# Interleaved channels and a plain load of x in a convolution and gated feed-forward kernel on Trainium2

## The chip, the cores and the metric

The kernel runs on one core of one Trainium2 chip. The metric is the time of one execution on the device in microseconds (us), the median of several runs. The profile belongs to one further execution; its span runs from the first to the last instruction.

## The reference

The input x has 8 sequences of 4096 tokens with 192 channels. Eight heads of 24 channels each have seven taps, made positive and normalised by a softmax. Each channel is convolved along the tokens, causally, with its head's taps. The result goes through two matrix products with an activation between them, 192 to 2048 to 192:

```python
w = weight - np.max(weight, axis=-1, keepdims=True)
w = np.exp(w)
w = w / (np.sum(w, axis=-1, keepdims=True) + 1e-09)
x_pad = np.concatenate([np.zeros((B, K - 1, D)), x], axis=1)
x_unf = x_pad[:, idx, :].reshape(B, S, K, H, group)     # idx[s, k] = s + k
x = np.einsum('hk,bskhg->bshg', w, x_unf).reshape(B * S, D)
h = x @ w_in
g = h * (1.0 / (1.0 + np.exp(-beta * h)))
out = g @ w_out
```

All inputs and the output are float32; 32768 tokens in all.

## The kernel before

The tokens are cut into two streams of 16384 (NS = 2). Stream 0 lies on partitions 0 to 63, stream 1 on 64 to 127, so that a 64-row matmul of one stream runs beside one of the other. The 192 channels are three groups (NK = 3) of 64: group `kk` holds channels 64 kk to 64 kk + 63.

The work goes in steps over the tokens of both streams: 128, 128, 256, and then 31 steps of 512. A tile `j` is 512 tokens; the first three steps share tile 0. Step `i` runs 16 units (NF = 16 blocks of 128 hidden channels). In each unit `mm1` makes one block of h for step i (six matmuls, L257) and ScalarE's Silu writes it to `g` (L259), while `mm2` adds a share of the output of step i - 1 (L293), in an order laid out by `mm2_plan`. When a pair of 128-token blocks is complete, `store` copies it from PSUM on VectorE (L301, `o_sb`, four buffers) and SP stores it (L307). A step of 512 has four such pairs, complete near 6/16, 8/16, 14/16 and 16/16 of the following step. `last` does the second product of the last step alone (L316).

VectorE makes the convolution of step i + 1 during step i, two operations per unit from a list (`conv_ops`): a copy of the six last tokens of the tile before (`halo`, L220), then for each tap k and group kk one operation over n tokens, a multiply for k = 0 (L229) and a multiply-add for the others (L231); the last writes `xc` in bfloat16. The multiplier is a column of `taps3`, for which the head masks and sums the normalised taps of all heads.

x comes by `load_x`: eight DMAs per tile on POOL's queue, which cast to bfloat16 and put groups and streams in order (`x_bf`, three buffers). `transpose_x` issues four DMA transposes per tile on SP's queue (L104) into `xt`, three buffers, channels on partitions. Both are called at the start of a step: the transposes of tile j + 2, then the load of tile j + 3. Every DMA queue and every engine keeps the order of the program.

The head loads the first 128 tokens in float32 (`x0`), multiplies them with the taps on VectorE (L168) and sums seven shifted diagonal matmuls (L185) on TensorE for the `xc` of step 0. `w_in` is loaded with a cast by POOL's queue: columns 0 to 511 for both halves of the partitions, of the rest one half each, which SP's queue then copies to the other half (`copy_w_in`, L84). `w_out` is loaded in four parts and scaled by 1/beta on POOL (L207).

Of the kernel before, what the change touches and what calls it, by code (L numbers as in the profile page):

```python
# [10 lines left out]
FP32 = mybir.dt.float32  # L11
BF16 = mybir.dt.bfloat16
# [6 lines left out]
def kernel(  # L19
# [14 lines left out]
    group = D // H  # L34
# [3 lines left out]
    NK = D // 64  # L38
    NS = 2
    TS = B * S // NS  # L40
    TILE = 512

# [8 lines left out]
    xbf_pool = ctx.enter_context(tc.tile_pool(name="xbf", bufs=3))  # L51
# [13 lines left out]

    x0 = consts.tile([128, NS, D], FP32, name="x0")
    pin(nc.sync.dma_start(out=x0, in_=xs[:, 0:128, :].rearrange("s p d -> p s d")))
    wbc = consts.tile([128, H, K], FP32, name="wbc")
    pin(nc.sync.dma_start(out=wbc, in_=weight.rearrange("h k -> (h k)").partition_broadcast(128)))
    beta16 = consts.tile([NF, 128], FP32, name="beta16")  # L70
    pin(nc.sync.dma_start(out=beta16, in_=moe_beta.rearrange("(c p) -> c p", p=128)))

    w_in_s = consts.tile([128, NK, F], BF16, name="w_in_s")
    w_in_v = moe_w_in.rearrange("(k c) f -> c k f", c=64)
# [4 lines left out]
    def load_w_in(half, f0, f1):  # L79
        pin(nc.gpsimd.dma_start(out=w_in_s[64 * half:64 * half + 64, :, f0:f1], in_=w_in_v[:, :, f0:f1]))  # L80

    def copy_w_in(half, f0, f1):
        o = 1 - half
        pin(nc.sync.dma_start(out=w_in_s[64 * o:64 * o + 64, :, f0:f1],  # L84
                              in_=w_in_s[64 * half:64 * half + 64, :, f0:f1]))

    xbf_of, xt_of = {}, {}

    def load_x(j, b0=0, b1=4):
        if j not in xbf_of:  # L90
            xbf_of[j] = xbf_pool.tile([128, 4, NK, NS, 64], BF16, name="x_bf")
        t = xbf_of[j]
        for b in range(b0, b1):
            for s in range(NS):
                src = xs[s, TILE * j + 128 * b:TILE * j + 128 * (b + 1), :]
                pin(nc.gpsimd.dma_start(out=t[:, b, :, s, :],  # L96
                                        in_=src.rearrange("p (k c) -> p k c", c=64)))

    def transpose_x(j, b0=0, b1=4):
        if j not in xt_of:  # L100
            xt_of[j] = xt_pool.tile([128, NK, LEAD + TILE], BF16, name="xt")
        for b in range(b0, b1):
            c = LEAD + 128 * b
            pin(nc.sync.dma_start_transpose(  # L104
                out=xt_of[j][:, :, c:c + 128],
                in_=xbf_of[j][:, b, :, :, :].rearrange("p k s c -> p (k s c)")))

# [7 lines left out]


    load_w_in(0, 0, 512)
    load_w_in(1, 0, 512)
    shift = consts.tile([128, 128 + PAD], BF16, name="shift")
    pin(nc.gpsimd.memset(shift, 0.0))  # L120
    pin(nc.gpsimd.affine_select(out=shift, in_=shift, compare_op=ALU.not_equal, fill=1.0,
                                base=PAD, pattern=[[-1, 128 + PAD]], channel_multiplier=1))
# [4 lines left out]
    load_x(0, 0, 4)  # L127
    mask = consts.tile([128, NK, H], FP32, name="mask")
    pin(nc.gpsimd.memset(mask, 1.0))
    for s in range(NS):  # L130
        m = mask[64 * s:64 * s + 64, :, :]
        pin(nc.gpsimd.affine_select(out=m, in_=m, compare_op=ALU.is_ge, fill=0.0, base=0,  # L132
                                    pattern=[[64, NK], [-group, H]], channel_multiplier=1))
        pin(nc.gpsimd.affine_select(out=m, in_=m, compare_op=ALU.is_ge, fill=0.0, base=group - 1,  # L134
                                    pattern=[[-64, NK], [group, H]], channel_multiplier=-1))
    load_w_in(0, 512, 1024)
    load_w_in(1, 1024, 1536)
    load_w_in(0, 1536, 2048)
    load_x(1)

    for c in range(0, NF, 4):
        pin(nc.sync.dma_start(out=w_out_f[:, c:c + 4, :], in_=w_out_v[:, c:c + 4, :]))  # L142
        if c == 0:
            transpose_x(0, 0, 2)
            copy_w_in(0, 512, 1024)
        if c == 4:
            copy_w_in(1, 1024, 1536)
            transpose_x(0, 2, 4)
        if c == 8:
            copy_w_in(0, 1536, 2048)  # L150


    mx = consts.tile([128, H], FP32, name="mx")
    pin(nc.vector.tensor_reduce(out=mx, in_=wbc, axis=AX.X, op=ALU.max))
    pin(nc.vector.tensor_tensor(wbc, wbc, mx[:, :, None].to_broadcast([128, H, K]), ALU.subtract))
    pin(nc.scalar.activation(wbc, wbc, AF.Exp))
    pin(nc.scalar.activation(scrap, one, AF.Silu))
    sm = consts.tile([128, H], FP32, name="sm")
    pin(nc.vector.tensor_reduce(out=sm, in_=wbc, axis=AX.X, op=ALU.add))
    rs = consts.tile([128, H], FP32, name="rs")  # L160
    pin(nc.vector.reciprocal(rs, sm))
    taps = consts.tile([128, H, K], FP32, name="taps")
    pin(nc.vector.tensor_tensor(taps, wbc, rs[:, :, None].to_broadcast([128, H, K]), ALU.mult))


    xw = consts.tile([128, K, NS, D], BF16, name="xw")
    for k in range(K):
        pin(nc.vector.tensor_tensor(  # L168
            xw[:, k, :, :].rearrange("p s (h c) -> p s h c", c=group),
            x0.rearrange("p s (h c) -> p s h c", c=group),  # L170
            taps[:, None, :, k:k + 1].to_broadcast([128, NS, H, group]),
            ALU.mult))

    warm = psum_h.tile([128, 2, TILE], FP32, name="ph")
    for i in range(8):
        pin(nc.tensor.matmul(warm[:, i % 2, :], zeros[:, 0:128], zeros, start=True, stop=True))  # L176
    bps = psum_h.tile([128, 2, TILE], FP32, name="ph")
    pin(nc.tensor.transpose(bps[:, 0, 0:NF], beta16, id16))
    cva = psum_o.tile([128, 2, TILE], FP32, name="po")
    cvb = psum_o.tile([128, 2, TILE], FP32, name="po")  # L180
    cv = [cva[:, 0, 0:128], cva[:, 1, 0:128], cvb[:, 0, 0:128]]
    for k in range(K):
        for kk in range(NK):
            for s in range(NS):
                pin(nc.tensor.matmul(cv[kk][64 * s:64 * s + 64, :], xw[:, k, s, 64 * kk:64 * kk + 64],  # L185
                                     shift[:, k:k + 128], start=(k == 0), stop=(k == K - 1)))
    xc_of = {}
    xc_of[0] = xc_pool.tile([128, NK, TILE], BF16, name="xc")
    for kk in range(NK):
        pin(nc.scalar.activation(xc_of[0][:, kk, 0:128], cv[kk], AF.Copy))  # L190
# [6 lines left out]
    tmp3 = consts.tile([128, NK, K, H], FP32, name="tmp3")  # L197
    for kk in range(NK):
        pin(nc.vector.tensor_tensor(tmp3[:, kk, :, :],
                                    mask[:, kk:kk + 1, :].to_broadcast([128, K, H]),  # L200
                                    taps.rearrange("p h k -> p k h"), ALU.mult))
    taps3 = consts.tile([128, NK, K], FP32, name="taps3")
    pin(nc.vector.tensor_reduce(out=taps3, in_=tmp3, axis=AX.X, op=ALU.add))


    for c in range(NF):
        pin(nc.gpsimd.tensor_scalar_mul(w_out_s[:, c, :], w_out_f[:, c, :], rbeta[:, c:c + 1]))  # L207


    def conv_ops(i):  # L210
        t0, n = steps[i]
        j, c0 = t0 // TILE, t0 % TILE
        ops = []

        def halo():
            xt = xt_of[j]
            if t0 % S == 0 or t0 == 128:
                pin(nc.vector.memset(xt[:, :, LEAD - PAD:LEAD], 0.0))
            elif c0 == 0:
                pin(nc.vector.tensor_copy(xt[:, :, LEAD - PAD:LEAD], xt_of[j - 1][:, :, TILE + LEAD - PAD:]))  # L220

        def tap(kk, k):
            xt, xc = xt_of[j], xc_of[i]
            acc = accs[i]
            src = xt[:, kk, LEAD - PAD + c0 + k:LEAD - PAD + c0 + k + n]
            w = taps3[:, kk, k:k + 1]
            a = acc[:, kk, 0:n]
            if k == 0:
                pin(nc.vector.tensor_scalar_mul(a, src, w))  # L229
            else:  # L230
                pin(nc.vector.scalar_tensor_tensor(  # L231
                    out=xc[:, kk, 0:n] if k == K - 1 else a, in0=src, scalar=w, in1=a,
                    op0=ALU.mult, op1=ALU.add))

        def begin():
            xc_of[i] = xc_pool.tile([128, NK, TILE], BF16, name="xc")
            accs[i] = acc_pool.tile([128, NK, TILE], FP32, name="acc")
            if c0 == 0 or t0 == 128:
                halo()

        ops.append(begin)
        for k in range(K):
            for kk in range(NK):
                ops.append(lambda kk=kk, k=k: tap(kk, k))
        return ops

    accs, g_of, po_of = {}, {}, {}

    def mm1(i, fc):
        n = steps[i][1]
        ph = psum_h.tile([128, NS, TILE], FP32, name="ph")
# [69 lines left out]
    for i in range(n_steps):  # L323
# [3 lines left out]
        j = steps[i][0] // TILE  # L327
        if i == 1:
            transpose_x(1)
            load_x(2)  # L330
        elif i == 2:
            transpose_x(2)
            load_x(3)
# [44 lines left out]
```

## Time and profile before

| | |
|---|---|
| median of 3 runs | 715.21 us (714.91 to 715.98) |
| profiled execution | 712.91 us |
| its span | 711.2 us |
| granted TensorE clock | 0.999 |
| PE / ACT / DVE / POOL busy | 687.7 / 578.8 / 502.2 / 218.2 us |
| share of the 16 DMA engines, first four slices and after | 0.9 or more, then about 0.5 |

PE is TensorE, PEld its weight load, DVE VectorE, ACT ScalarE, POOL GpSimd, SP SyncE. A small q marks the engine's sequencer, which issues DMAs. In a group of instructions the columns are line, engine, operation, output <- inputs, shapes, count, then busy time and mean duration in ns, then idle time just before them and what ended it. In the list of waits they are the total, the number and the longest.

### The profile page before, as it was taken

The page shows a single profiled execution, that of the slowest core. Times are in us where ns is not written, and L with a number is a line of the kernel's source. Part 1 is how long each engine was busy: PE and PEld are TensorE (multiplying, and loading weights), DVE is VectorE, ACT ScalarE, POOL GpSimd, SP SyncE. Part 2 cuts the span into 40 slices and gives each one's busy share as a digit, 9 for nine tenths or more (in the row PEclk, how much of TensorE's full clock was granted, in tenths as well). Part 3 has the DMA queues.
Part 4 walks back from the last instruction along what each step waited for, and adds up shares of the span by engine and source line. Part 5 has one row for each costly group of instructions (what it writes and reads, how often), then busy time and mean ns, then how long its engine had stood idle before and what let it go on. Part 6 is the DMA issues. An engine that isn't in the chain of part 4 may idle for free.

```text
span 711.2 us, 25346 instructions
## 1 busy us (share of the span) xinstructions
PE 687.7 (97%) x11379; PEld 524.5 (74%) x11379; DVE 502.2 (71%) x877; ACT 578.8 (81%) x552; POOL 218.2 (31%) x290
## 2 busy tenths in 40 slices
PE   5589999999999999999999999999999999999998
PEld 2466777777777777777777777777777777777777
DVE  4779776677687667678667768766776876676702
ACT  3489888888888888888888888888888888888882
POOL 9997332223333113333212333321233330000000
PEclk9999999999999999999999999999999999999999
DMA  9999554455555445555445555544555553221012
GB/s 132 149 95 96 81 88 69 72 84 79 75 80 87 69 73 85 75 72 87 79 71 78 74 74 81 88 71 71 83 80 74 80 85 64 58 62 52 28 44 68
DMA packets 194861, 55.38 MB, mean 78 GB/s; under 512 B 158128, under 2 KB 194752, under 8 KB 194752
## 3 DMA queue, kind: packets, MB, share of 16 engines
q0 software_dynamic: 103440, 13.58, 30.6%
q1 hardware_dynamic: 91312, 40.17, 22.3%
q8 instruction: 89, 1.46, 0.9%
q14 instruction: 20, 0.16, 0.1%
HBM read 28.94 MB, written 25.17 MB: 76 GB/s over the span
## 4 chain that ended last, share of the span: by engine, by line
PE 93%; POOL 2%; DMA 2%; DVE 2%; issue 0%; ACT 0%; SPq 0%; DVEq 0%; POOLq 0%
PE ph L257 46%; PE po L293 46%; PE po L316 2%; DVE acc L231 1%; POOL x_bf L96 1%; DMA w_in_s<-w_in_s 1%; DMA x_bf<-in_x_dram 1%; POOL w_in_s L80 0%; ACT g L259 0%; DVE xc L231 0%; DVE acc L229 0%; SPq L142 0%; POOL mask L132 0%; POOL mask L134 0%; DVE o_sb L320 0%
## 5 line engine op out<-in xcount | busy, mean ns | idle before, releaser
L259 ACT ACTIVATE g<-ph,beta 128x1024 bf16<-128x1024 f32 (+2 forms) x544 | 574.9, 1064 | 111.8 <-PE ph L257 107.4
L257 PE MATMUL ph<-xc,w_in_s 64*128 64x512 bf16 (+2 forms) x3264 | 432.7, 367 | 17.0 <-DMA w_in_s<-w_in_s 9.4
L293 PEld LDWEIGHTS <-g 64*128 64x128 bf16 x7936 | 359.6, 94 | 101.5
L293 PE MATMUL po<-w_out_s,g 64*128 64x192 bf16 x7936 | 422.4, 243 | 0.0
L231 DVE SCALAR_TENSOR_TENSOR acc<-xt,taps,acc 128x512 f32<-128x512 bf16 (+2 forms) x495 | 326.7, 727 | 0.0
L96 POOL DMA_DIRECT2D x_bf<-in_x_dram x256 | 197.5, 774 | 366.7 <-DMA xt<-x_bf 349.4
L257 PEld LDWEIGHTS <-w_in_s 64*128 64x128 bf16 x3264 | 168.2, 96 | 74.6 <-DMA w_in_s<-w_in_s 10.5
L301 DVE COPY o_sb<-po 128x384 f32<-128x384 f32 x124 | 68.9, 556 | 183.5 <-PE po L293 183.5
L231 DVE SCALAR_TENSOR_TENSOR xc<-xt,taps,acc 128x512 bf16<-128x512 bf16 (+2 forms) x99 | 66.5, 727 | 0.0
L229 DVE TENSOR_SCALAR acc<-xt,taps 128x512 f32<-128x512 bf16 (+2 forms) x99 | 41.8, 481 | 9.2 <-DMA xt<-x_bf 8.1
L207 POOL TENSOR_SCALAR w_out_s<-w_out_f,rbeta 128x192 bf16<-128x192 f32 x16 | 15.6, 992 | 0.1
L316 PE MATMUL po<-w_out_s,g 128*128 128x192 bf16 x128 | 10.7, 246 | 0.0
L316 PEld LDWEIGHTS <-g 128*128 128x128 bf16 x128 | 10.5, 98 | 0.2 <-issue 0.2
L320 DVE COPY o_sb<-po 128x192 f32<-128x192 f32 x8 | 2.9, 358 | 7.6 <-PE po L316 7.6
L176 PE MATMUL ph<-zeros 128*128 128x512 bf16 x8 | 3.6, 631 | 1.2 <-DVE one L112 1.2
L220 DVE COPY xt<-xt 128x18 bf16<-128x18 bf16 x28 | 4.6, 166 | 0.0
L185 PE MATMUL po<-shift,xw 128*64 128x128 bf16 x42 | 3.3, 314 | 1.2 <-DVE xw L168 1.2
L185 PEld LDWEIGHTS <-xw 128*64 128x64 bf16 x42 | 2.0, 152 | 2.4 <-DVE xw L168 2.4
L80 POOL DMA_DIRECT2D w_in_s<-in_moe_w_in_dram x5 | 3.3, 665 | 0.8 <-POOLq L362 0.8
L168 DVE TENSOR_TENSOR xw<-x,taps 128x384 bf16<-128x384 f32 x7 | 3.4, 553 | 0.0
L176 PEld LDWEIGHTS <-zeros 128*128 128x128 bf16 x8 | 1.0, 140 | 2.9 <-issue 1.7
L190 ACT ACTIVATE xc<-po 128x128 bf16<-128x128 f32 x3 | 0.6, 278 | 3.1 <-PE po L185 3.1
(30 smaller groups left out, 8.8 us busy)
## 6 DMA issues: line engine op xcount, KB each, us to landing
out_dram<-o_sb SPq DMA_DIRECT2D x124, 192.0 KB, 2.3
x_bf<-in_x_dram POOLq DMA_DIRECT2D x256, 48.0 KB, 3.1
xt<-x_bf SPq DMA_TRANSPOSE x128, 2.3
w_out_f<-in_moe_w_out_dram SPq DMA_DIRECT2D x4, 384.0 KB, 6.7
w_in_s<-in_moe_w_in_dram POOLq DMA_DIRECT2D x5, 192.0 KB, 5.5
out_dram<-o_sb SPq DMA_DIRECT2D x8, 96.0 KB, 1.6
w_in_s<-w_in_s SPq DMA_DIRECT2D x3, 192.0 KB, 6.8
x<-in_x_dram SPq DMA_DIRECT2D x1, 192.0 KB, 2.6
```

The costliest lines, as they stand in the source:

```text
L96: pin(nc.gpsimd.dma_start(out=t[:, b, :, s, :], in_=src.rearrange("p (k c) -> p k c", c=64)))
L176: pin(nc.tensor.matmul(warm[:, i % 2, :], zeros[:, 0:128], zeros, start=True, stop=True))
L185: pin(nc.tensor.matmul(cv[kk][64 * s:64 * s + 64, :], xw[:, k, s, 64 * kk:64 * kk + 64], shift[:, k:k + 128], start=(k == 0), stop=(k == K ...
L207: pin(nc.gpsimd.tensor_scalar_mul(w_out_s[:, c, :], w_out_f[:, c, :], rbeta[:, c:c + 1]))
L220: pin(nc.vector.tensor_copy(xt[:, :, LEAD - PAD:LEAD], xt_of[j - 1][:, :, TILE + LEAD - PAD:]))
L229: pin(nc.vector.tensor_scalar_mul(a, src, w))
L231: pin(nc.vector.scalar_tensor_tensor(out=xc[:, kk, 0:n] if k == K - 1 else a, in0=src, scalar=w, in1=a, op0=ALU.mult, op1=ALU.add))
L257: pin(nc.tensor.matmul(ph[:, s, 0:n], w_in_s[r, kk, ts(fc, 128)], xc_of[i][r, kk, 0:n], start=(kk == 0), stop=(kk == NK - 1)))
L259: pin(nc.scalar.activation(g_of[i][:, fc, :, 0:n], ph[:, :, 0:n], AF.Silu, scale=beta[:, fc:fc + 1]))
L293: pin(nc.tensor.matmul(po[:, q, 0:D], g_of[i][r, fc, s, ts(b, 128)], w_out_s[r, fc, :], start=(phase == 0 and fc == 0), stop=(phase == 1 a ...
L301: pin(nc.vector.tensor_copy(o_sb, po[:, :, 0:D]))
L316: pin(nc.tensor.matmul(po[:, 0, 0:D], g_of[i][:, fc, s, ts(b, 128)], w_out_s[:, fc, :], start=(fc == 0), stop=(fc == NF - 1)))
```

## The change

Group `kk` now holds channels kk, kk + 3, kk + 6 and so on, so that partition q of a stream holds channels 3q, 3q + 1, 3q + 2, which belong to one head. One column of taps per partition then serves all three groups, and a tap becomes one VectorE operation over [128, 3, n]. The rows of `w_in` are read in the same interleaved order. The taps are loaded with one row per partition, exponentiated with a running sum, and normalised as `tapn`; the masks go.

x is loaded as float32, two DMAs per tile on SP's queue (for the first 256 tokens on ACT's queue), and cast and reordered on VectorE (`cast_x`, two operations per tile). Transposes stay on SP's queue; they are issued after the casts, at the end of VectorE's list of the step, and the load of the next tile comes behind them. The list of a step is spread over 14 units. In a steady step VectorE's order is: halo, two taps, first output copy, two taps, second output copy, three taps, two casts, third and fourth output copy. SP's is: three stores, four transposes, two loads, the fourth store.

The first 256 tokens are transposed on TensorE. The first 128 are convolved there: seven diagonal matrices of unnormalised taps in the 4-byte type fp32r, 21 matmuls, and ScalarE scales by the reciprocal of the sum as it copies. `w_in` columns 512 to 1023 are loaded for both halves, so two copies are left, and half of `w_out` is scaled on VectorE. The order of the loads in the head changes with it.

```diff
-    NK = D // 64
+    NK = 3
+    Q = D // NK
...
-    xbf_pool = ctx.enter_context(tc.tile_pool(name="xbf", bufs=3))
+    xf_pool = ctx.enter_context(tc.tile_pool(name="xf", bufs=2))
+    xbf_pool = ctx.enter_context(tc.tile_pool(name="xbf", bufs=2))
...
-    def load_x(j, b0=0, b1=4):
-        for b in range(b0, b1):
-            for s in range(NS):
-                src = xs[s, TILE * j + 128 * b:TILE * j + 128 * (b + 1), :]
-                pin(nc.gpsimd.dma_start(out=t[:, b, :, s, :],
-                                        in_=src.rearrange("p (k c) -> p k c", c=64)))
+    def load_x(j, s, b0=0, b1=NB, eng=None):
+        src = xs[s, TILE * j + 128 * b0:TILE * j + 128 * b1, :]
+        pin((eng or nc.sync).dma_start(out=xf_of[j][:, s, b0:b1, :],
+                                       in_=src.rearrange("(b p) d -> p b d", p=128)))
+
+    def cast_x(j, s, b0=0, b1=NB):
+        pin(nc.vector.tensor_copy(
+            xbf_of[j][:, b0:b1, :, s, :].rearrange("p b k q -> p k b q"),
+            xf_of[j][:, s, b0:b1, :].rearrange("p b (q k) -> p k b q", k=NK)))
...
-    w_in_v = moe_w_in.rearrange("(k c) f -> c k f", c=64)
+    w_in_v = moe_w_in.rearrange("(q k) f -> q k f", k=NK)
...
+    pin(nc.scalar.activation(etap, taps, AF.Exp, bias=nmax, accum_out=tsum))
+    for s in range(NS):
+        cast_x(0, s, 0, 2)
+    for k in range(K):
+        pin(nc.vector.tensor_scalar_mul(diag[:, k, :], ident, etap[:, k:k + 1]))
+    pin(nc.vector.tensor_scalar_mul(tapn, etap, rsum))
...
+    for b in range(2):
+        for kk in range(NK):
+            pin(nc.tensor.transpose(tr[:, b, kk, :],
+                                    xbf_of[0][:, b, kk, :, :].rearrange("p s q -> p (s q)"), ident))
+    pin(nc.scalar.activation(xr[:, :, PAD:], tr[:, 0, :, :], AF.Copy))
...
-            for s in range(NS):
-                pin(nc.tensor.matmul(cv[kk][64 * s:64 * s + 64, :], xw[:, k, s, 64 * kk:64 * kk + 64],
-                                     shift[:, k:k + 128], start=(k == 0), stop=(k == K - 1)))
+            pin(nc.tensor.matmul(cv[kk], diag[:, k, :], xr[:, kk, k:k + 128],
+                                 start=(k == 0), stop=(k == K - 1)))
...
-        def tap(kk, k):
-            src = xt[:, kk, LEAD - PAD + c0 + k:LEAD - PAD + c0 + k + n]
-            w = taps3[:, kk, k:k + 1]
-            a = acc[:, kk, 0:n]
+        def tap(k):
+            c = LEAD - PAD + c0 + k
+            src = xt_of[j][:, :, c:c + n]
+            a = accs[i][:, :, 0:n]
+            w = tapn[:, k:k + 1]
...
+    def extra_ops(i):
+        if i == 0:
+            ops += [lambda c=c: scale_w_out(c, nc.vector) for c in range(8)]
...
+        elif i > 2:
+            nxt = j + 2
+            for s in range(NS):
+                ops.append(lambda s=s: cast_x(nxt, s))
+            def go():
+                for b in range(NB):
+                    transpose_x(nxt, b)
+                if (nxt + 1) * TILE < TS:
+                    for s in range(NS):
+                        load_x(nxt + 1, s)
+            ops.append(go)
...
     for i in range(n_steps):
-        elif i > 2:
-            if (j + 2) * TILE < TS:
-                transpose_x(j + 2)
-            if (j + 3) * TILE < TS:
-                load_x(j + 3)
+            dve = dve + ex
         for u in range(NF):
             mm1(i, u)
             for t in plan[u]:
                 mm2(i - 1, *t)
-            for op in conv[:2]:
+            upto = len(dve) * (u + 1) // (NF - 2)
+            for op in dve[done:upto]:
                 op()
+            done = max(done, upto)
```

The second tile's casts and transposes are put in step 0, the third's in step 1. Lines L211, L235, L237, L250, L81 and L92 of the changed kernel are the scaling of `w_out`, the opening multiply, the multiply-add, `mm1`'s matmuls, the cast and the transpose.

## The prediction

> **What bounds the kernel now.** I read the page first, then a table of stages, then the waits, then one steady step in the order of time, first VectorE, then SyncE's queue. The page:
>
> ```profile
> PE 687.7 (97%) x11379; PEld 524.5 (74%) x11379; DVE 502.2 (71%) x877; ACT 578.8 (81%) x552; POOL 218.2 (31%) x290
> L231 DVE SCALAR_TENSOR_TENSOR acc<-xt,taps,acc 128x512 f32<-128x512 bf16 (+2 forms) x495 | 326.7, 727 | 0.0
> L301 DVE COPY o_sb<-po 128x384 f32<-128x384 f32 x124 | 68.9, 556 | 183.5 <-PE po L293 183.5
> ```
>
> TensorE is busy 97% of the span, and VectorE's copies of the result wait for TensorE, never the other way. The table of stages (length, then busy time of PE, PEld, DVE, ACT, POOL):
>
> ```profile
> 200.00:220.92 20.92, 20.92 (x358) 16.01 (x354) 15.42 (x28) 17.83 (x16) 6.16 (x8) 1.00 0.51 78
> 500.00:520.92 20.92, 20.92 (x356) 16.01 (x352) 15.35 (x27) 17.83 (x17) 5.75 (x8) 1.00 0.50 77
> ```
>
> A steady step of 512 tokens per stream lasts 20.92 us and TensorE is busy through all of it. The change leaves these matmuls as they are, so no steady step can get shorter; it can only get longer. The waits:
>
> ```profile
> PE ph L257 <- DMA w_in_s<-w_in_s: 9.4, 3, 5.7
> DVE acc L229 <- DMA xt<-x_bf: 8.1, 2, 4.1
> PE ph L257 <- DVE xc L231: 3.1, 3, 2.6
> PE ph L257 <- DMA w_in_s<-in_moe_w_in_dram: 2.1, 1, 2.1
> ```
>
> All that TensorE loses to waits lies in the head: 11.5 us for `w_in` and its copies, 3.1 us for the first large convolution. VectorE waited for a transpose only twice, both times in the head. One steady step (start, length, engine, line):
>
> ```profile
> 216.36 0.56 DVE L301 COPY o_sb<-po 128x384 f32<-128x384 f32 x1 [2.06 <-PE po L293]
> 216.83 0.16 DVE L220 COPY xt<-xt 128x18 bf16<-128x18 bf16 x1
> 217.03 1.28 DVE L229 TENSOR_SCALAR acc<-xt,taps 128x512 f32<-128x512 bf16 x3
> 218.22 4.06 DVE L231 SCALAR_TENSOR_TENSOR acc<-xt,taps,acc 128x512 f32<-128x512 bf16 x6
> ...
> 231.10 2.07 DVE L231 SCALAR_TENSOR_TENSOR xc<-xt,taps,acc 128x512 bf16<-128x512 bf16 x3
> ```
>
> ```profile
> 216.94 0.37 SPq L307 DMA_DIRECT2D out_dram<-o_sb  x1
> 217.42 5.38 SPq L104 DMA_TRANSPOSE xt<-x_bf  x4
> 224.79 13.45 SPq L307 DMA_DIRECT2D out_dram<-o_sb  x4
> ```
>
> The step begins at 216.3. VectorE convolves at once, on an `xt` that was transposed a whole step earlier, and has `xc` ready 16.9 us into a step of 20.92. The four transposes leave at the start of the step and have some 20 us until they are used.
>
> **The steady step after the change.** Per tile the 64 small loads-with-cast on POOL's queue go for good (8 issues of 0.77 us a step; POOL held nobody, gain nothing); two loads on SP's queue take their place, behind the transposes and ahead of the fourth store of the step: 0.4 us of issue each (a store's issue), covered by four `o_sb` buffers, else 0.8 us a step. Twenty-one taps of 512 become seven of 1536, each reading the accumulator that the one before it wrote. Two casts of 128x768 come last in VectorE's list of the step. The transposes of that tile wait for both casts, and in SP's order they stand behind the store of the third output pair, whose copy VectorE does after the casts. The first tap of the next step waits for all four transposes. So a loop appears, from taps to casts to transposes to taps, with all of it in series:
>
> - Taps. A tap of 512 takes 0.746 us alone, and follows its predecessor every 0.661; one of 128 takes 0.338, every 0.264. So a tap is n/0.96 ns, plus 0.21 to its end or 0.13 to the next start. At 1536: 1.81, or 1.73. A dependent operation starts 0.04 after the end of its source (5.19 + 0.21 to 5.44 at the reduction of the taps in the head): 1.85. The multiply that opens the chain is 0.482 at 512, every 0.395, half the time per element: 1.06 with the dependence. Two output copies between taps add 0.47 each, but then the tap behind them need not wait. From first tap to the first cast: 1.06 + 1.73 + 0.47 + 1.85 + 1.73 + 0.47 + 1.85 + 1.85 + 1.73 = 12.74. (By itself the convolution falls from 13.3 to about 12.4, off the path before.)
> - Casts, not in the trace. Nearest row: the opening multiply (one source, SBUF to SBUF, 16 and 32 bit): 768 elements at its rate are 0.40 + 0.13 = 0.53. At the rate of the taps 0.93. I take 0.53, since that row has the same kind of operands, and keep 0.93: 1.06 or 1.86 for two. A gain is excluded, there was no cast on VectorE before.
> - Hand-over. Output copy 0.56 (its length), 0.03 to the store's issue, 0.48 from there to the first transpose (216.94 to 217.42). From its start to the landing of the fourth: median 6.95 over tiles 4 to 31, 6.2 to 8.4 (issues 1.3 apart, the last lands 2.3 after its issue, an odd one 1 us late). 0.1 to the first tap. Sum 8.1. POOL's loads came only after the transposes, so their absence does not shorten this.
>
> Loop: 12.74 + 1.06 + 8.12 = 21.9 us against 20.92. It does not fit under the matmuls, and TensorE, which needs the whole of `xc` for its first matmul, waits 1.0 us in each step.
>
> [...]
>
> **The head.** Before: first large matmul at 10.9, the small steps held by `w_in` until 29.1, and the first large step's `xc` complete at 53.86. After: the softmax chain loses its subtraction and three small products. Two transposed blocks and a 0.3 to 0.5 us copy come ahead of the first convolution. The 21 fp32r matmuls cost between 0.11 each (pairs of the old diagonal matmuls) and 0.43 (the one 4-byte matmul in the trace, 0.256 + 0.177): 2.3 to 9.1 us, I take 6 between them. The first real matmul so moves to about 14. That is covered: units 8 to 15 wait for two copies of `w_in`. POOL now issues all six `w_in` loads by 6.2 (the last three were issued at 11 to 13); landing in order at some 1.5 us each they end near 14, and copies that took 6 to 8 us land near 20 instead of 29. Without that cover the 3 us would count in full. The first small step ends near 23 instead of 31. Most of this is then lost: SP's queue puts three `w_out` loads and the second tile's x behind those copies (landing about 23), then come two casts, the convolution of 256 (7.0 us, to 31.5), a cast of the third tile that waits for loads queued behind four transposes (to 36), an output copy, and the 12.4 us of the first large convolution. `xc` is complete at 49.5, 4.4 us earlier than before. Bounds: 8 us earlier if the loads land as they did at their fastest, 2 later if as at their slowest.
>
> **The sum.** The second large convolution starts at 50.0, its casts end at 64, its transposes land at 71.1. From there 28 rounds of 21.9 to the last tile's first tap: 684.3. Then 12.9 to its `xc`, 20.9 for its step, and 13.7 that lay behind that step before (711.2 - 697.5): span 731.8, against 711.2. The profiled execution was 712.91, 1.7 over its span, and the median of the runs is 2.3 more, 715.21: so 735.8 for a median, I say 735. A tenth of a microsecond in the loop is 2.8 in the time.
>
> **The rivals.**
> 1. The casts run at the taps' rate, 0.93 each. Loop 22.7, 29 casts' worth of 0.8 more: span 755, median 759. For it: nothing in the trace reads in steps of three floats. Against it: the opening multiply's halved rate. Chance 0.26.
> 2. Faster: the loop fits under the 20.92. That needs 1 us off 21.9: transposes that land within 6.2, as in the best rounds, and taps that follow each other at 0.66-like spacing in spite of their dependence (0.5). Then only the head counts: 711.2 - 4.4 = 706.8, median about 711. The point from which it decides is a loop of 21.16, where 28 rounds eat the head's gain. For it: the smallest landings in the trace, seven of 28 tiles under 6.6. Against it: the median of 6.95, and a needed coincidence. Chance 0.13.
> 3. The head's reordering does not help (later `w_in`, slow fp32r): 6 us on top of the forecast, 741; it lies inside its range.
>
> The forecast, with a loop of 21.4 to 22.3 and the head's bounds, is 718 to 750, chance 0.61 with the third rival in it. About 0.2% can be told from no change here. Faster by more 0.12, within 0.03, slower 0.85. The range of 717 to 762 takes in the slow casts and leaves out the fitting loop.
>
> **What would show it.** Right: VectorE idle before L235 for `xt`, near 6.8 us a step and some 190 in all; TensorE idle before L250 for `xc` L237, about 1 us a step, 25 in all; steps of 21.9; POOL idle after the head. Casts (L81) of 0.6 us say forecast, 1.0 say rival 1. First real matmul near 14, first `xc` of 512 near 49.5. Wrong: TensorE busy throughout steps of 20.92, or L235 seldom waiting.

## The result

The changed kernel takes 774.03 us (median, 772.21 to 775.72) against 715.06 us (714.49 to 715.98) for the kernel before in the same runs: 1.0823 times as long, with a 95% interval of 1.0796 to 1.085. The forecast of 735 us with a range of 717 to 762 had the direction right and the size wrong. The profiled execution of the changed kernel took 774.04 us and its span is 772.3 us, so its parts can be held against the forecast span of 731.8 us. The kernel before was profiled in its fastest execution on record (712.91 us; its other runs took 714.38 to 721.01 us).

The page of the kernel after, busy time first, then the chain of work that ended last:

```profile
PE 700.8 (91%) x11364; PEld 527.0 (68%) x11364; DVE 519.5 (67%) x485; ACT 580.1 (75%) x554; POOL 11.2 (1%) x22
...
DVE 37%; SPq 20%; issue 18%; DMA 15%; PE 8%; POOL 0%; DVEq 0%; POOLq 0%
```

TensorE, 97% busy before, is 91% busy, and it holds only 8% of the chain. VectorE, SP's queue and the DMAs carry the chain now, although VectorE is busy for no more than 67%: a chain that runs through three engines needs none of them full. The groups of the tap operations, the cast and the second product, shapes kept apart:

```profile
L235 DVE TENSOR_SCALAR acc<-xt,tapn 128x1536 f32<-128x1536 bf16 x31 | 56.2, 1812 | 195.1 <-DMA xt<-xb 195.0
L81 DVE CAST xb<-xf 128x768 bf16<-128x768 f32 x62 | 49.8, 842 | 8.1 <-DMA xf<-in_x_dram 8.1
L287 PE MATMUL po<-w_out_s,g 64*128 64x192 bf16 x7936 | 423.1, 243 | 49.9 <-DVE o_sb L295 49.5
```

The opening multiply lasts 1812 ns. The forecast had it at 1.01 us, half the time per element of the other taps. A cast lasts 842 ns. VectorE waits 195.0 us before the multiply for the transposes. The list of waits (total, number, longest):

```profile
DVE acc L235 <- DMA xt<-xb: 195.0, 29, 7.7
...
PE po L287 <- DVE o_sb L295: 49.5, 48, 1.4
...
PE ph L250 <- DVE xc L237: 9.9, 3, 6.7
DVE xb L81 <- DMA xf<-in_x_dram: 8.4, 5, 4.2
...
DVE nmax L148 <- DMA taps<-in_weight_dram: 6.7, 1, 6.7
```

TensorE's loss of 49.5 us stands at `mm2`, which waits for VectorE to empty an output buffer in PSUM (L295), and not at `mm1`, which takes `xc`. One steady step, VectorE's order and then SP's queue:

```profile
330.30 1.81 DVE L235 TENSOR_SCALAR acc<-xt,tapn 128x1536 f32<-128x1536 bf16 x1 [6.27 <-DMA xt<-xb]
332.15 1.82 DVE L237 SCALAR_TENSOR_TENSOR acc<-xt,tapn,acc 128x1536 f32<-128x1536 bf16 x1
333.88 0.55 DVE L295 COPY o_sb<-po 128x384 f32<-128x384 f32 x1
...
343.83 1.59 DVE L81 CAST xb<-xf 128x768 bf16<-128x768 f32 x2
345.35 1.15 DVE L295 COPY o_sb<-po 128x384 f32<-128x384 f32 x2
346.42 0.16 DVE L226 COPY xt<-xt 128x18 bf16<-128x18 bf16 x1
353.46 1.81 DVE L235 TENSOR_SCALAR acc<-xt,tapn 128x1536 f32<-128x1536 bf16 x1 [6.88 <-DMA xt<-xb]
```

```profile
345.92 0.37 SPq L301 DMA_DIRECT2D out_dram<-o_sb  x1
346.34 5.89 SPq L92 DMA_TRANSPOSE xt<-xb  x4
```

This is the loop of the forecast, in its order: taps from 330.30 to 343.83, two casts to 345.35, the third output copy, its store at 345.92, four transposes from 346.34, and the next tile's first tap at 353.46. It takes 23.16 us here. From tile 3 (77.81) to tile 31 (723.38) the 28 rounds take 23.06 us each. The table of stages gives TensorE's share of this step (columns as before):

```profile
346.00:369.16 23.16, 21.27 (x356) 15.95 (x354) 16.09 (x15) 17.83 (x17) 0.00 (x0) 1.00 0.31 87
```

TensorE is busy 21.27 of 23.16 us at a granted clock of 1.00: the matmuls are the old ones, and the rest is waiting.

### The profile page after: what moved, and what is told of

It reads as the page before. It is cut to its first block, busy times and chain, and to the rows that moved or that the text cites. A ratio compares the mean times of both kernels' runs of the same rounds, so it can differ in the third digit from the quotient of the medians.

```text
span 772.3 us, 24542 instructions
## 1 busy us (share of the span) xinstructions
PE 700.8 (91%) x11364; PEld 527.0 (68%) x11364; DVE 519.5 (67%) x485; ACT 580.1 (75%) x554; POOL 11.2 (1%) x22
## 4 chain that ended last, share of the span: by engine, by line
DVE 37%; SPq 20%; issue 18%; DMA 15%; PE 8%; POOL 0%; DVEq 0%; POOLq 0%
DVE acc L237 21%; SPq L92 18%; DMA xt<-xb 7%; DMA xf<-in_x_dram 6%; DVE o_sb L295 6%; DVE xb L81 6%; DVE acc L235 4%; PE ph L250 4%; PE po L287 3%; DMA w_in_s<-in_moe_w_in_dram 1%; PE po L310 1%; SPq L301 1%; SPq L75 1%; DVE xc L237 1%; DMA w_out_f<-in_moe_w_out_dram 0%
## 5 line engine op out<-in xcount | busy, mean ns | idle before, releaser
L287 PEld LDWEIGHTS <-g 64*128 64x128 bf16 x7936 | 358.5, 94 | 163.3 <-issue 65.9
L287 PE MATMUL po<-w_out_s,g 64*128 64x192 bf16 x7936 | 423.1, 243 | 49.9 <-DVE o_sb L295 49.5
L250 PE MATMUL ph<-xc,w_in_s 64*128 64x512 bf16 (+2 forms) x3264 | 433.9, 368 | 12.7 <-DVE xc L237 9.9
L237 DVE SCALAR_TENSOR_TENSOR acc<-xt,tapn,acc 128x1536 f32<-128x1536 bf16 (+2 forms) x165 | 289.4, 1754 | 3.8
L250 PEld LDWEIGHTS <-w_in_s 64*128 64x128 bf16 x3264 | 168.2, 96 | 69.9 <-DVE xc L237 10.5
L235 DVE TENSOR_SCALAR acc<-xt,tapn 128x1536 f32<-128x1536 bf16 (+2 forms) x33 | 57.4, 1740 | 195.1 <-DMA xt<-xb 195.0
L295 DVE COPY o_sb<-po 128x384 f32<-128x384 f32 x124 | 68.2, 550 | 23.0 <-PE po L287 21.6
L237 DVE SCALAR_TENSOR_TENSOR xc<-xt,tapn,acc 128x1536 bf16<-128x1536 bf16 (+2 forms) x33 | 58.0, 1758 | 1.6 <-DVE acc L237 0.5
L81 DVE CAST xb<-xf 128x768 bf16<-128x768 f32 (+1 forms) x66 | 51.6, 819 | 8.4 <-DMA xf<-in_x_dram 8.4
L211 POOL TENSOR_SCALAR w_out_s<-w_out_f,rbeta 128x192 bf16<-128x192 f32 x8 | 6.4, 811 | 16.2 <-DMA w_out_f<-in_moe_w_out_dram 16.2
L186 PE MATMUL po<-xr,diag 128*128 128x128 f32 x21 | 4.7, 418 | 0.5 <-ACT xr L178 0.5
L186 PEld LDWEIGHTS po<-xr,diag 128*128 128x128 f32 x21 | 4.6, 331 | 0.6 <-ACT xr L178 0.6
L148 DVE TENSOR_REDUCE nmax<-taps 128x1 f32<-128x7 f32 x1 | 0.2, 159 | 6.7 <-DMA taps<-in_weight_dram 6.7
L211 DVE TENSOR_SCALAR w_out_s<-w_out_f,rbeta 128x192 bf16<-128x192 f32 x8 | 2.1, 316 | 2.9 <-DMA w_out_f<-in_moe_w_out_dram 2.8
```

Of the source, the lines that this page charges most:

```text
L81: pin(nc.vector.tensor_copy(xbf_of[j][:, b0:b1, :, s, :].rearrange("p b k q -> p k b q"), xf_of[j][:, s, b0:b1, :].rearrange("p b (q k) -> ...
L186: pin(nc.tensor.matmul(cv[kk], diag[:, k, :], xr[:, kk, k:k + 128], start=(k == 0), stop=(k == K - 1)))
L211: pin(eng.tensor_scalar_mul(w_out_s[:, c, :], w_out_f[:, c, :], rbeta[:, c:c + 1]))
L237: pin(nc.vector.scalar_tensor_tensor(out=xc_of[i][:, :, 0:n] if k == K - 1 else a, in0=src, scalar=w, in1=a, op0=ALU.mult, op1=ALU.add))
L250: pin(nc.tensor.matmul(ph[:, s, 0:n], w_in_s[half_of(s), kk, ts(fc, 128)], xc_of[i][half_of(s), kk, 0:n], start=(kk == 0), stop=(kk == NK ...
L287: pin(nc.tensor.matmul(po[:, q, 0:D], g_of[i][r, fc, s, ts(b, 128)], w_out_s[r, fc, :], start=(phase == 0 and fc == 0), stop=(phase == 1 a ...
```

## The experiments

The theory: the time is lost in the loop of taps, casts and transposes in series, longer than forecast because the multiply and the casts run slower. The rivals: the long tap operations delay VectorE's output copies and so starve TensorE of PSUM buffers, loop or no loop; or the head carries a good part of the loss. Each experiment is two runs of its kernel, e1 ten and e8 six, and each loop is read from one profiled execution.

**Casts at the start of the list (e1).** The casts and the transposes come ahead of the taps of the step, so that the transposes have a step's time. The operations stay the same, and so does the number of copies behind long taps.

```diff
-            dve = dve + ex
+            dve = (ex + dve) if i > 2 else (dve + ex)
...
             upto = len(dve) * (u + 1) // (NF - 2)
+            if i > 2 and ex:
+                upto = min(len(dve), max(len(dve) * (u + 1) // (NF - 4), 7))
```

> In the steady steps the two casts and the four transposes of a tile come first in VectorE's and SP's lists instead of last; same operations, same order elsewhere. Loop theory (taps, casts, transposes, taps in series set the step of 23.06 us): the transposes now have most of a step to land, so steps go back to 20.92 us, VectorE stops waiting for xt before L235, and 28 x 2.1 us go: about 714 us, within 1% of the kernel before. Rival (TensorE waits because the output copies stand behind 1.8 us taps and so free the two PSUM output buffers late; L287 waited 49.5 us for L295): the copies stand behind as many or more taps as now, steps stay near 23 us, 770 us or more.

Measured: 715.19 us against 715.39, ratio 0.9983 (0.9957 to 1.0009), and steps of 20.92 us. A steady step of it, and the same groups:

```profile
300.00:320.92 20.92, 20.92 (x354) 16.03 (x352) 16.46 (x15) 17.83 (x17) 0.00 (x0) 1.00 0.35 96
```

```profile
L287 PE MATMUL po<-w_out_s,g 64*128 64x192 bf16 x7936 | 423.2, 243 | 0.3 <-POOL w_out_s L211 0.3
L235 DVE TENSOR_SCALAR acc<-xt,tapn 128x1536 f32<-128x1536 bf16 x31 | 56.2, 1813 | 1.1
```

The multiply is as slow as in the changed kernel, 1813 ns, and its wait of 195.0 us is gone; so is TensorE's wait for output copies. In VectorE's list the first output copy of a step now stands behind two casts and three taps, the third behind four taps. VectorE reaches them early all the same, and waits for TensorE:

```profile
DVE o_sb L295 <- PE po L287: 143.6, 69, 7.3
```

So the rival of the late copies falls: in the changed kernel they were where the loop's wait showed, not its cause. In this order the same slow operations cost nothing; the whole loss hangs on the place of the casts and transposes.

**The old kernel with late transposes (e7).** The reverse: the kernel before, with nothing changed but the point from which the transposes of the steady steps are issued.

```diff
-            if (j + 2) * TILE < TS:
-                transpose_x(j + 2)
...
+            if u == 13 and i > 2 and (j + 2) * TILE < TS:
+                transpose_x(j + 2)
```

> The kernel before, with one edit: in the steady steps the four transposes of tile j + 2 are issued late in the step, behind the third output pair's store, as the changed kernel does, instead of at its start. Loads, taps and head are those of before. Loop theory: 21 taps and two copies take 14.0 from the first tap, then 0.56 + 0.03 + 0.48 + 6.95 + 0.1 until the next: a loop of 22.1, 28 x 1.2 us over 20.92, about 748. Rival (the long taps, the casts or the loads on SP's queue are what makes the steps longer): 715.

Measured: 760.73 us, ratio 1.0634 (1.0611 to 1.0658), a loop of 22.55 us (tile 3 at 77.9 to tile 31 at 709.4). Its waits:

```profile
DVE acc L229 <- DMA xt<-x_bf: 166.1, 31, 6.6
...
PE po L293 <- DVE o_sb L301: 34.3, 55, 2.1
```

Short taps, no casts, loads on POOL's queue, and yet the same two waits in the same places. Late transposes alone cost the old kernel 45 us; the whole change costs 59. The loop was 0.45 us longer than expected: over the 28 rounds the mean from the first tap to the third copy is 14.2 us, not 14.0, and from the first transpose to the next first tap 7.3, not 7.05.

**The multiply's output in rows (e2).** The output `acc[:, :, 0:512]` fills its tile, so it is one run of 1536, while the input is three rows of 512. A wider tile makes both three rows.

```diff
-            accs[i] = acc_pool.tile([128, NK, TILE], FP32, name="acc")
+            accs[i] = acc_pool.tile([128, NK, TILE + 16], FP32, name="acc")
```

> The accumulator tile gets 16 unused columns per group, so that the opening multiply's output is 3 rows of 512 like its input and no longer one run of 1536. Theory: it ran at 1 element per cycle (1.81 us) because output and input no longer had the same outermost size; it falls to about 1.0 us, the loop from 23.06 to 22.25, the time by 23 us to about 751. Rival (an operation of this length or type is that slow whatever its shape): 1.81 us and 774 us as before. The rival of the late output copies expects hardly a change.

Measured: 759.8 us, ratio 1.0598 (1.0528 to 1.0669), and a loop of 22.52, 0.54 shorter.

```profile
L235 DVE TENSOR_SCALAR acc<-xt,tapn 128x1536 f32<-128x1536 bf16 x31 | 39.8, 1285 | 195.0 <-DMA xt<-xb 194.9
```

The multiply fell by 0.53 us, from 1812 to 1285 ns, and the loop by as much: the multiply is in the loop. It did not fall to the 1.0 us expected. With the 0.96 elements per ns that the forecast drew from the taps of before (746 ns at 512, 338 at 128), 1812 ns is 1536/0.96 and 0.21 us of fixed cost, and 1285 ns is the same cost and about two thirds of the rest, not half.

**The cast's read in sequence (e3).** The cast reads each row of floats in order, not every third one.

```diff
-            xf_of[j][:, s, b0:b1, :].rearrange("p b (q k) -> p k b q", k=NK)))
+            xf_of[j][:, s, b0:b1, :].rearrange("p b (k q) -> p k b q", k=NK)))
```

> The cast reads the floats of a group in sequence instead of every third one; the channels then go to the wrong groups, so the output is another one, with the same amount of work. Theory (the step of 12 bytes costs): a cast falls from 0.84 to about 0.61 us, one to the next from 0.76 to 0.53, the loop by 0.46 to 22.6, the time by 13 us to 761. Rival (a cast from 32 to 16 bit in four dimensions has this price anyway): 0.84 and 774.

Measured: 765.49 us, ratio 1.0678 (1.0601 to 1.0755), a loop of 22.72, 0.34 shorter.

```profile
L81 DVE CAST xb<-xf 128x768 bf16<-128x768 f32 x62 | 39.9, 683 | 7.0 <-DMA xf<-in_x_dram 7.0
```

One cast follows the other after 0.60 us where it took 0.76. So the step of three floats costs 0.16 us in a cast of 768; the loop lost both casts' worth.

**Outermost size even (e5).** The multiply is written with two halves of the tokens outermost, the cast with its four blocks outermost and not its three groups. The tiles lie in memory as in the changed kernel. The run tests whether it is the three groups outermost that cost the time, so that two or four outermost cost less.

```diff
-            xbf_of[j][:, b0:b1, :, s, :].rearrange("p b k q -> p k b q"),
-            xf_of[j][:, s, b0:b1, :].rearrange("p b (q k) -> p k b q", k=NK)))
+            xbf_of[j][:, b0:b1, :, s, :].rearrange("p b k q -> p b k q"),
+            xf_of[j][:, s, b0:b1, :].rearrange("p b (q k) -> p b k q", k=NK)))
...
-                pin(nc.vector.tensor_scalar_mul(a, src, w))
+                pin(nc.vector.tensor_scalar_mul(a.rearrange("p k (h n) -> p h k n", h=2),
+                                                src.rearrange("p k (h n) -> p h k n", h=2), w))
```

> The changed kernel with the same elements in another order: the cast goes over blocks first (4 outermost instead of 3), the opening multiply over two halves of the tokens first (2 outermost instead of 3, or instead of 1536 against 3). The padded accumulator gave 1.285 us and the contiguous cast 0.60 from one to the next, which are 2/3 of 1536 and of 768 at 0.96 per ns plus 0.21 and 0.07. [...] Rival (these rates are those of the length, or of the step of 12 bytes alone): the multiply stays at 1.29 to 1.81, the cast at 0.76, 759 to 774 us.

Measured: 743.16 us, where the author's estimate was 744, ratio 1.0389 (1.0369 to 1.0408), a loop of 21.99.

```profile
L235 DVE TENSOR_SCALAR acc<-xt,tapn 128x1536 f32<-128x1536 bf16 x31 | 31.6, 1020 | 186.8 <-DMA xt<-xb 186.7
L81 DVE CAST xb<-xf 128x768 bf16<-128x768 f32 x62 | 39.7, 680 | 7.6 <-DMA xf<-in_x_dram 7.6
```

The multiply has the 1.02 us that the forecast gave it, and the loop of 21.99 stands beside the 21.92 forecast. A multiply of the same 1536 numbers takes 1812, 1285 or 1020 ns by the shape in which they are written down.

**Transposes ahead of the third store (e4), and with the even shapes (e6).** The second cast and the transposes become one entry of the list, so that no output copy and no store come between them.

```diff
-            for s in range(NS):
-                ops.append(lambda s=s: cast_x(nxt, s))
+            ops.append(lambda: cast_x(nxt, 0))

             def go():
+                cast_x(nxt, 1)
                 for b in range(NB):
                     transpose_x(nxt, b)
...
             ops.append(go)
+            ops.append(lambda: None)
```

> The transposes are issued right behind the second cast in SP's order, ahead of the third output pair's store, instead of behind it. Loop theory: the copy (0.54), its way to SP (0.03) and the store's issue (0.42) leave the loop, 23.06 becomes 22.06, 28 us go, about 746. Rival of the late output copies: no change, 774; a rival in which the DMA engines are what delays xt: no change either, since as much moves in as little time.

Measured: 749.69 us, ratio 1.0457 (1.0387 to 1.0527), a loop of 22.23, 0.83 shorter, where 1.0 was expected. The second experiment adds the shapes of e5:

> Even outermost sizes and transposes ahead of the third store together. Loop theory: the terms add, 23.06 - 1.06 - 0.82 = 21.2, so 28 x 1.88 us go, about 721; TensorE's wait for the output copies falls under 10 us. A rival in which several waits overlap and hide each other: less than the sum, 730 or more.

Measured: 723.59 us, ratio 1.0115 (1.0084 to 1.0146), a loop of 21.30. From 23.06, the 1.07 of e5 and the 0.83 of e4 would leave 21.16; the 1.06 in the sum of the expectation was the author's estimate, for which e5 gave 1.07. The two terms add, within 0.14, as they do in a chain without a second one beside it; the two runs of this kernel, 721.26 and 725.93 us, lie 0.17 us a round apart, and the profile is of the longer. TensorE's wait for output copies is down to 7.9 us, as expected. The second rival of the forecast, the loop that fits, is nearly met here, and the kernel is still 1.2% slower than before. The point of 21.16 that the forecast named for it counted on a gain in the head that did not come.

**Casts first, even shapes, earlier loads in the head (e8).** The edits of e1 and e5, and the second and third tile's loads moved forward on SP's queue, past the loads of `w_out` and past four transposes.

```diff
+    for s in range(NS):
+        load_x(1, s)
...
-        load_x(1, s)
-    for s in range(NS):
...
             def go():
+                if i == 0:
+                    for s in range(NS):
+                        load_x(nxt + 1, s)
...
-                if (nxt + 1) * TILE < TS:
+                if i > 0 and (nxt + 1) * TILE < TS:
```

> Casts and transposes first in the step, even outermost sizes, and in the head the loads of the second tile ahead of w_out's and of the third ahead of the second's transposes. Loop theory: steady steps of 20.92 as in the run with the casts first. The head: VectorE waited 8 us for xf there, so the first xc of 512 is complete near 47 instead of 53.8 and the time falls by 5 to 7 us, to 708 to 710, about 1% below the kernel before. Rival (the head's end is set by the load of w_in and w_out, which now come later): 715 or more.

Measured: 712.58 us against 715.58, ratio 0.9955 (0.9938 to 0.9972): faster than both kernels, and 0.45% under the one before. The steps are 20.92 us, so all of the gain lies in the head, where the first large convolution begins at 38.83 and not at 40.62. It is 2.6 to 4.6 us short of what was expected. The waits for `xf` are gone, but VectorE now waits longer for `w_out`, whose loads were moved back and whose scaling stands ahead of the casts in its list:

```profile
DVE w_out_s L211 <- DMA w_out_f<-in_moe_w_out_dram: 7.3, 1, 7.3
```

In the changed kernel this wait is 2.8 us. So the first cast of the second tile begins at 25.93, no earlier than the 25.64 there. POOL's half of the scaling is late too, and TensorE waits for it:

```profile
L288 PE MATMUL po<-w_out_s,g 64*128 64x192 bf16 x7936 | 424.6, 244 | 3.1 <-POOL w_out_s L211 3.1
```

VectorE in turn waits 2.3 us for TensorE before its first output copy. The first `xc` of 512 comes into use at 51.50, not near 47. The rival, the loads that now come later, is right in part.

## Why the forecast was right and wrong

**What bounds the kernel: right.** No steady step got shorter in any run, and the best one, e8, is bound by the same 20.92 us.

**The loop and its order: right.** In the step shown it goes tap by tap and queue by queue as the forecast laid it out. Held against the step that begins at 330.30:

| Part | forecast | this step |
|---|---|---|
| first tap to first cast | 12.74 | 13.53 (330.30 to 343.83) |
| two casts | 1.06 | 1.52 (to 345.35) |
| third copy, store, transposes, to the first tap | 8.12 | 8.11 (to 353.46) |
| loop | 21.92 | 23.16 |

**The step that failed: the opening multiply, "half the time per element".** The row of before that it was scaled from is one group of 512 tokens: one run in, one run out. At [128, 3, 512] in and one run of 1536 out it went at 1536/0.96 + 0.21 = 1.81 us, the time per element of the other taps (1814 ns), 0.79 longer than taken, and the forecast's range had no bound for that. Over 28 rounds this is 22 us of the 40.5 that the span was off. The casts below are 13 more, and the hand-over gives 3 back. The size of the operation was scaled, its shape was not looked at. e2 and e5 show that the shape decides, and that 28 rounds follow it.

By that estimate (0.96 elements per ns and 0.21 us, from the taps of before) the three measured times are shares of one time: 3 rows against one run of 1536, all of it (1812 ns); 3 against 3, two thirds, 1536 x 2/3 / 0.96 + 0.21 = 1.28 (1285 ns); 2 against 2, half, 0.80 + 0.21 = 1.01 (1020 ns). What in VectorE makes these shares is not shown.

**Casts: between forecast and first rival.** 0.76 us from one to the next, where the forecast had 0.53 and the rival 0.93. Two causes, both shown: the three outermost groups, and the read of every third float, whose removal alone gave 0.16 us in 768 elements (e3); why that read costs is not shown. With four blocks outermost the strided cast also follows after 0.59 (e5). Why not after the 0.53 of the same rate is not settled: the strided read may cost these 0.06 there too, but an even shape read in sequence was not tried.

**Dependent taps: right.** 1.81 us each, the next 0.04 after the end (330.30 + 1.81 to 332.15), 1.73 to a copy (332.15 to 333.88). From start to start that is the 1.85 us of the forecast, 0.12 more than to a copy. What the 0.12 consists of is not shown: no run here has the same taps without their dependence. The loop of 21.4 at the lower end of the forecast's range is shown by no run either; the loop of the changed kernel took 23.06.

**Hand-over: right** to 0.01 us in the step shown; the mean of the 28 rounds is 8.01 us, 0.11 below the forecast. e4 took 0.83 us off the loop by the order of two entries.

**Where TensorE would wait: wrong in name.** The forecast put the wait at `mm1` (L250) for `xc`, "25 in all". It was 9.9 there, 9.6 of it in the head, and 49.5 at `mm2` (L287) for PSUM buffers. VectorE idles while it waits for the transposes, and does the copies of a step only between and behind its taps; both come from the same loop, and e1 removes both.

**The head: the gain of 4.4 us did not come.** The forecast's clock for tile 3's first tap was 71.1, the measured one 77.8. Of these 6.7, 4.6 lie before the second large convolution (54.62 against 50.0) and 2.1 in its round. The softmax chain began late, as its tap load landed late (6.7 us of waiting before L148), and the first real matmul came at 15.4, not 14. The fp32r matmuls took 4.7 us, within their bounds and less than the 6 taken:

```profile
L186 PE MATMUL po<-xr,diag 128*128 128x128 f32 x21 | 4.7, 418 | 0.5 <-ACT xr L178 0.5
```

Step 0 then ended at 24.2, against the 31.2 of before: the cover by `w_in` was as forecast. What ate it were the casts, which waited for `xf`: tile 1's until 25.6 and 27.9, tile 2's until 38.0 and 39.2. The first large `xc` was complete for TensorE at 54.09, against 53.86 before. The queue ahead of the loads was seen, and their landing put 2 to 5 us too early ("landing about 23", "to 36"). e8 supports this in part: with earlier loads the waits for `xf` are gone and the head gives 3 us, though a wait for `w_out` takes their place at the second tile's casts.

**The sum.** 28 rounds of 23.06 in place of 21.9 are 32.4 us, the head 6.7, the end (48.9 against 47.5) 1.4: 40.5, which is 772.3 - 731.8.

**The rivals.** The slow casts at 759 had the price of the loop nearly right for a partly wrong reason. The fitting loop did not come; it comes when the casts and transposes are first in the step. The third, a head that does not help, came nearly in size (6.7 us for its 6), but `w_in` and the fp32r matmuls, which it named, were not the cause. The "64 small loads" per tile of the forecast are eight (256 in 32 tiles); the sum does not use them.

## What to carry to other kernels

Where a change moves a step of a pipeline from one step ahead to the same step, write down the loop that closes and sum it in series: busy shares showed nothing of it here, where VectorE, 67% busy, was the largest part of the chain that set the time (37%). Put the work that others wait for first in an engine's list and its own bulk behind it; that reordering alone was worth 59 us here. When a row's rate is scaled to a bigger operation, carry over its shape too, the number of rows on both sides (1812, 1285 and 1020 ns for one multiply here), and write bounds for the case that the fast rate does not hold.

## What was not expected of the hardware

A merge of three operations into one can lose its speed: three multiplies of 512 took 3 x 0.395 = 1.19 us by their spacing before, one of 1536 took 1.81, and 1.02 once it was written with two halves outermost.

The granted clock fell after waits in the head, most after the longest ones: to 0.55 after 6.7 us in the changed kernel, to 0.53 after 8.2 us in e1. The stage of 54 to 58 us, after, in e1, and before (length, busy time of PE, PEld, DVE, ACT, POOL, clock, DMA share, GB/s):

```profile
54.00:58.00 4.00, 3.91 (x32) 2.06 (x33) 3.93 (x5) 1.59 (x2) 0.00 (x0) 0.55 0.18 53
```

```profile
54.00:58.00 4.00, 4.00 (x32) 2.26 (x30) 3.93 (x6) 1.91 (x2) 0.00 (x0) 0.53 0.30 78
```

```profile
54.00:58.00 4.00, 4.00 (x58) 2.60 (x56) 3.96 (x9) 3.65 (x4) 4.00 (x6) 1.00 1.18 130
```

TensorE waited 6.7 us for `xc` until 54.09 after the change, 8.2 us until 53.78 in e1, and 2.6 us until 52.54 before. In the first two it did 32 matmuls in these 4 us, not 58. In e1 the first large step began about when the last part of `xc` was complete in the kernel before (53.86), and ended about 2 us later (71.99 against 69.84), which is most of the difference of the spans (713.4 against 711.2). The medians of the two kernels do not differ (715.19 and 715.39).

In the next stage after the change, some 4 us after the matmuls began again, the clock is 1.00:

```profile
58.00:62.00 4.00, 4.00 (x58) 2.60 (x56) 3.92 (x3) 4.00 (x5) 0.00 (x0) 1.00 0.00 0
```

Shorter waits also went with a lower clock, 0.72 and 0.58, in two places, one after the change and one in e8:

```profile
36.00:42.00 6.00, 5.78 (x80) 4.94 (x77) 3.61 (x5) 4.43 (x7) 0.00 (x0) 0.72 0.47 144
```

```profile
30.00:36.00 6.00, 4.34 (x66) 3.76 (x67) 5.69 (x7) 2.75 (x7) 2.08 (x2) 0.58 0.26 52
```

Ahead of the first TensorE had waited 2.9 us (until 35.81). Around the start of the second it waited four times for `w_out`, 3.1 us in all and 1.2 at the longest. The 2.6 us before left the clock at 1.00, and in e1 it was 1.00 from 30 to 36 us, of which TensorE was idle for 2.2 us, and in the 6 us behind. So the length of the longest wait alone does not settle it here; what does is open.
